# Sums of weight blocks moved to the second pass, and attention loads issued apart, in a fused attention and mixture-of-experts kernel

## The chip, the cores and the metric

One Trainium2 chip, of which the kernel uses one core. The time is that of one execution of the whole program on the device, in microseconds (us), the median of the runs shown. Engines: TensorE (PE in the profile), VectorE (DVE), ScalarE (ACT), GpSimd (POOL) and SyncE (SP), which here issues DMAs only. GpSimd issues DMAs too, from a queue of its own.

## What is computed

Attention within chunks of 64 tokens (batch 4, 8 heads, 576 tokens, head size 64), whose output is 2304 rows of 512 numbers; then two mixture-of-experts layers over these rows. The first sends every row through all four experts, weighted by given probabilities; the second sends each row through the one of eight experts that its logits choose.

```python
attn = softmax(scale * q_c @ k_c.T) ; x = attn @ v_c            # 64-token chunks, 8 heads
p = domain_probs / domain_probs.sum(-1)                          # first layer, E = 4
x = sum(p[:, e:e+1] * (relu(x @ w1[e]) @ w2[e]) for e in range(4))
e = argmax(x @ w_gate) ; g = softmax(x @ w_gate)[e]              # second layer, E = 8
out = g * (relu(x @ w1[e]) @ w2[e])                              # F = 1024, D = 512
```

## The kernel before

**Numbers as pairs.** Every operand of the large products is split into a high part (`wh`, `xh`, `hh`, cast by ScalarE to fp32r) and a low part (`wl`, `xl`, `hl`, the remainder, by VectorE); a product is three matmuls. A weight chunk is 128 x 1024: 512 columns of w1 and 512 of w2. It is loaded by SyncE into one of four raw buffers (`load_next`, L339), copied by ScalarE (L388) and subtracted by VectorE (L389) into one of eight pairs (`split_next`, L382). `feed` (L409) is called once per chunk or third of a unit: it issues the loads that have a free buffer and one or two splits. All orders are those of the program: each engine and each DMA queue works its list in order, and an instruction that waits holds up all behind it.

**Passes.** The 18 tiles of 128 rows go in five groups of 2, 4, 4, 4 and 4. The first pass (32 chunks, group 0) works the first layer plainly: per chunk a first product of 12 matmuls of 256 columns (L442 to L444) and a second one of 6 of 512 columns (L502), one chunk or two later. The four later passes use a scheme with seven products instead of eight (`unit`, L1011): 16 units per pass, each with three chunks, called kinds: kind 0 holds blocks of the weights themselves, kind 1 four sums and differences of them, kind 2 two chunks of w2. A unit has 42 matmuls of 256 columns (L1006) and 24 of 512 (L1094); the latter are woven into the next unit. GpSimd adds one pair of partial results in each (L1057).

**The sums.** `w_sums` (L371) is called in the first pass after every second split. GpSimd makes four sums of 128 x 256 from two raw chunks (L376 to L379) into `scr` or `xsum` and stores them to the DRAM tensor `wsum` (L380, 512 KB, GpSimd's queue). In all four later passes kind 1 is loaded from `wsum`. Since the sums read two raw chunks, loads in the first pass go in pairs: `done -= done % 2` (L418). At the pass's end GpSimd also makes the sums of the activations (`x_sums`, L284, L291), which ScalarE and VectorE split (`x_split`, L293).

**Attention** is done a group ahead, in pieces spread over the pass (`plan`, L948). `att_load` (L159) loads queries and keys of a tile (`atkq`, 512 KB, two buffers) and values (`atv`, 256 KB, four buffers). At the start tiles 0 to 3 are loaded; later, when the values of tile t are done, `attq` (L279) takes tile t + 4, due two calls of `feed` later, or at once in the first pieces, and both its loads are issued together (L923, L1032). A load whose buffer is not yet free waits on SyncE's queue.

**Routing.** Work beside the products stands in generators (`sides`), of which `side` (L909) takes a step at each call: `logits` (L523), then `route` (L559) with the exponential on ScalarE (L583), the ranks by a small matmul (L594), slot numbers on VectorE (L605) and an indirect store of each row's number and weight to `slots` by GpSimd (L608). In the last stage (the second layer, blocks of 256 rows, `step`, L1192, eight chunks each) the last group's routing and the tables (`tables`, `rest`: small matmuls L787 and L801, short VectorE instructions) take two steps per chunk in the first two blocks (L1216). In the second block, at its third chunk, SyncE fetches the slots of the next block (L845), two chunks later GpSimd gathers its rows (L850), and after the first product of the last chunk TensorE transposes them (`prep`, L861).

Of the kernel before, what the change touches and what calls it, by code (L numbers as in the profile page):

```python
# [9 lines left out]
F32 = mybir.dt.float32  # L10
# [4 lines left out]
ALU = mybir.AluOpType  # L15
# [3 lines left out]
P = 128  # L19
NT = 2304  # L20
NTILE = NT // P
# [35 lines left out]
LOWS = (9, 13)  # L57


@with_exitstack  # L60
def attn_moe_moe2(ctx, tc, att, probs, wg, wgt, w12, m2w, out):
# [94 lines left out]
    atin = {}  # L156
    attq = []

    def att_load(t, parts=((0, 1024), (1024, 1536))):  # L159
        if t not in atin:  # L160
            atin[t] = (
                apool.tile([P, 1024], F32, tag="atkq", name=f"atkq{t}", bufs=NKQ),
                apool.tile([P, 512], F32, tag="atv", name=f"atv{t}", bufs=NATT),
            )
        for c in parts:
            to = atin[t][0][:, c[0]:c[1]] if c[1] <= 1024 else atin[t][1]
            nc.sync.dma_start(out=to, in_=att[t, :, c[0]:c[1]])
# [29 lines left out]
    def att_scores(t, half):  # L197

        a = atin[t][0]
        if half == 0:  # L200
            live[t] = [
                sds[t % 2],
                apool.tile([P, 2, H], F32, tag="mx", name=f"mx{t}"),
                None,
            ]
        if half == 0 or t < GROUPS[0]:
            live[t][2] = ps("m").rearrange("p (h x) -> p h x", x=CH)
        sd, mx, sc = live[t]
        for g in range(4 * half, 4 * half + 4):
            for c in (slice(0, CH), slice(CH, P)):  # L210


                nc.tensor.matmul(
                    sc[other(c), g, :], lhsT=a[c, 512 + g * CH:512 + (g + 1) * CH], rhs=a[c, g * CH:(g + 1) * CH],
                    start=True, stop=True,
                )
            yield
        if heads(t, half):
            hs, n = heads(t, half)
            nc.vector.tensor_reduce(out=mx[:, 0, hs].unsqueeze(2), in_=sc[:, hs, :], axis=AX.X, op=ALU.max)  # L220
            nc.vector.tensor_tensor(
                out=sd[:, hs, 0:CH], in0=sc[:, hs, :], in1=mx[:, 0, hs].unsqueeze(2).to_broadcast([P, n, CH]),
                op=ALU.subtract,
            )
            nc.scalar.activation(sd[:, hs, 0:CH], sd[:, hs, 0:CH], AF.Exp, scale=0.125)

# [20 lines left out]
    def att_values(t, half, g):  # L247
        a = atin[t][1]
# [26 lines left out]
        if half == 1:  # L275
            live.pop(t)
            atin.pop(t)
            if t + NATT < NTILE:
                attq.append((t + NATT, stream["call"] + 2 if stream["call"] else 0))  # L279
# [4 lines left out]
    def x_sums(g):  # L284

        summed.append(g)
# [52 lines left out]
    def load_next():  # L339
# [28 lines left out]
    kept = []  # L368
    summed = []

    def w_sums(i, one, two):  # L371

        a11, a12, a21, a22 = one[:, 0:HN], one[:, HN:2 * HN], two[:, 0:HN], two[:, HN:2 * HN]
        to = (scr[:, 0:4, :], xsum.rearrange("p a k n -> p (a k) n")[:, 0:4, :])[0 if 1 in summed else i % 2]
        s1, s2, s3, s4 = [to[:, k, :] for k in range(4)]
# [4 lines left out]
        nc.gpsimd.dma_start(out=wsum[i * P:(i + 1) * P, :], in_=to.rearrange("p k n -> p (k n)"))  # L380

    def split_next():  # L382
# [4 lines left out]
        n = 768 if NPLAIN <= j < NM1 and (j - NPLAIN) % 3 == 0 else 1024  # L387
        nc.scalar.copy(wh[:, :n], raw[:, :n])  # L388
        lows.append(lambda: nc.vector.tensor_tensor(  # L389
            out=wl[:, :n], in0=raw[:, :n], in1=wh[:, :n].bitcast(F32), op=ALU.subtract  # L390
        ))
# [17 lines left out]
    def feed():  # L409
# [149 lines left out]
    def route(g, lg, wait):  # L559
# [359 lines left out]
    def chunk(j, x, sizes, fc, banks, frees, done, extra=()):  # L919
# [3 lines left out]
        while attq and attq[0][1] <= stream["call"]:  # L923
            att_load(attq.pop(0)[0])
# [24 lines left out]
    for g in range(1, len(GROUPS)):  # L949
        pcs = att_pieces(g)  # L950
        then = [lambda g=g: x_sums(g)] + [lambda g=g: x_split(g)] * (7 if g == 1 else 2)
# [59 lines left out]
    def unit(g, e, q, before, banks):  # L1011
# [19 lines left out]
        def extra(i):  # L1031
            while attq and attq[0][1] <= stream["call"]:  # L1032
                att_load(attq.pop(0)[0])
            feed()
            for p in plan.get(at + i, []):
                p()
            side()

        product(a, wa, 0, x["b11"], True, False)
# [20 lines left out]
        product(b, wa, HN, x["b21"], True, True)  # L1060
# [4 lines left out]
        product(a, wa, 2 * HN, x["t4"], False, True)  # L1065
# [40 lines left out]
    att_load(1, ((0, 1024),))  # L1106
    for t in range(2):
        att_load(t, ((1024, 1536),))
# [11 lines left out]
    for t in range(3, NATT):  # L1120
        att_load(t)
# [10 lines left out]
    for i, p in enumerate(pieces):  # L1132
# [5 lines left out]
        p()  # L1138
        keep_warm(WARM[1 + i])
# [52 lines left out]
    def step(s, c, sizes):  # L1192
# [11 lines left out]
        for fc in range(KF):  # L1204
# [6 lines left out]
            if s <= NFIRST:  # L1211
# [3 lines left out]
                else:  # L1215
                    side(2 if s < 2 else 1)  # L1216
# [84 lines left out]
```

## Time and profile before

| | |
|---|---|
| runs | 1181.06, 1181.13, 1183.89 us; median 1181.13 |
| profiled execution, its own time | 1183.33 us |
| its span, first to last instruction | 1181.3 us |
| TensorE busy | 1118.8 us, 95% of the span |
| VectorE, ScalarE, GpSimd busy | 761.4, 635.5, 255.3 us |
| mean granted TensorE clock | 0.98 of full speed |
| moved by DMA | 206.27 MB, 175 GB/s |

A busy TensorE is one that has matmuls in work; how fast they go depends on the clock granted, so a stretch is read with both. Idle time of an engine that is not the bottleneck costs nothing. The time behind an arrow in brackets is how long the engine stood idle before an instruction, and which instruction released it.

### The profile page before, as it was taken

The numbers are of one execution on the slowest core, as the hardware profiler recorded it, in microseconds if no ns is written. First come the engines' busy times: TensorE is split into PE (matmuls) and PEld (weight loads), VectorE is DVE, ScalarE is ACT, GpSimd is POOL, SyncE is SP. The second block draws the span as 40 slices with busy tenths as digits, with TensorE's granted clock in tenths as the row PEclk, the third lists the DMA queues.
The fourth block names the chain that finished last, engine by engine and source line by source line (L and its number), as shares of the span: only waits on it lengthen the run. The fifth ranks groups of instructions, "written<-read, shape, count | busy, mean of one in ns | idle before, by whom it ended". The sixth has DMA issues, their size and how long they took to land. (4 is left out here: it accounts for less than half of the span.)

```text
span 1181.3 us, 21164 instructions
## 1 busy us (share of the span) xinstructions
PE 1118.8 (95%) x7957; PEld 992.9 (84%) x7957; DVE 761.4 (64%) x1360; ACT 635.5 (54%) x1165; POOL 255.3 (22%) x291
## 2 busy tenths in 40 slices
PE   6699699999999999999999999999998999999996
PEld 4599589888888889898898898899986899788885
DVE  6577666576764666775665774675657566788871
ACT  3355356554655445555554565645444355677771
POOL 4476501000211200210210210120013111222220
PEclk9699999999999999999999999999999999999998
DMA  6688554534544464453344354354642486586850
GB/s 243 209 316 307 188 169 139 174 126 156 167 165 139 116 163 145 155 183 111 105 130 147 114 173 142 117 150 144 226 162 89 159 324 211 201 278 240 290 194 19
DMA packets 83905, 206.27 MB, mean 175 GB/s; under 512 B 13262, under 2 KB 22606, under 8 KB 83792
## 3 DMA queue, kind: packets, MB, share of 16 engines
q1 hardware_dynamic: 75536, 180.14, 46.3%
q0 software_dynamic: 8256, 24.67, 6.0%
q8 instruction: 65, 1.06, 0.4%
q14 instruction: 48, 0.39, 0.1%
HBM read 185.68 MB, written 20.27 MB: 174 GB/s over the span
## 5 line engine op out<-in xcount | busy, mean ns | idle before, releaser
L389 DVE TENSOR_TENSOR wl<-raw,wh 128x1024 fp32r<-128x1024 f32 (+1 forms) x276 | 332.5, 1206 | 120.8 <-ACT wh L388 120.7
L388 ACT CAST wh<-raw 128x1024 fp32r<-128x1024 f32 (+1 forms) x276 | 275.0, 997 | 28.5 <-DMA raw<-in_w 28.4
L1006 PE MATMUL ps_h<-xh,wh 128*128 128x256 f32 x896 | 258.7, 289 | 9.9 <-DVE hl L448 4.7
L1006 PE MATMUL ps_h<-xl,wh 128*128 128x256 f32 x896 | 253.3, 283 | 0.0
L1006 PE MATMUL ps_h<-xh,wl 128*128 128x256 f32 x896 | 252.6, 282 | 0.0
L1094 PE MATMUL ps_o<-wh,hh 128*128 128x512 f32 x512 | 201.5, 394 | 0.0
L1094 PE MATMUL ps_o<-wh,hl 128*128 128x512 f32 x512 | 201.5, 394 | 0.0
L1094 PE MATMUL ps_o<-wl,hh 128*128 128x512 f32 x512 | 201.0, 393 | 0.0
L1006 PEld LDWEIGHTS ps_h<-xh,wh 128*128 128x128 f32 x896 | 169.8, 189 | 24.6 <-ACT scr L1048 5.4
L1057 POOL TENSOR_TENSOR scr<-scr 128x256 f32<-128x256 f32 x64 | 58.1, 907 | 569.5 <-ACT scr L1056 569.3
L1006 PEld LDWEIGHTS ps_h<-xl,wh 128*128 128x128 f32 x896 | 169.5, 189 | 8.2
L1006 PEld LDWEIGHTS ps_h<-xh,wl 128*128 128x128 f32 x896 | 170.8, 191 | 0.0
L1068 ACT ACTIVATE hh<-scr 128x512 fp32r<-128x512 f32 (+1 forms) x128 | 66.7, 521 | 128.3 <-DVE scr L1061 126.1
L502 PE MATMUL ps_o<-wh,hh 128*128 128x512 f32 x328 | 124.6, 407 | 0.0
L1094 PEld LDWEIGHTS ps_o<-wh,hl 128*128 128x128 f32 x512 | 96.5, 188 | 21.6
L502 PE MATMUL ps_o<-wl,hh 128*128 128x512 f32 (+1 forms) x272 | 106.9, 397 | 0.0
L1094 PEld LDWEIGHTS ps_o<-wh,hh 128*128 128x128 f32 x512 | 97.1, 190 | 11.4
L1094 PEld LDWEIGHTS ps_o<-wl,hh 128*128 128x128 f32 x512 | 96.9, 189 | 11.2
L1069 DVE SCALAR_TENSOR_TENSOR hl<-scr,hh 128x512 fp32r<-128x512 f32 (+1 forms) x128 | 74.7, 584 | 44.8 <-ACT hh L1068 44.8
L1061 DVE TENSOR_TENSOR scr<-ps_h,scr 128x256 f32<-128x256 f32 x64 | 27.2, 424 | 93.9 <-PE ps_h L1006 93.8
L447 ACT ACTIVATE hh<-ps_h 128x256 fp32r<-128x256 f32 x80 | 30.7, 383 | 89.0 <-PE ps_h L444 83.0
L448 DVE SCALAR_TENSOR_TENSOR hl<-ps_h,hh 128x256 fp32r<-128x256 f32 x80 | 33.7, 421 | 66.0 <-ACT hh L447 64.3
(230 smaller groups left out, 1932.9 us busy)
## 6 DMA issues: line engine op xcount, KB each, us to landing
raw<-in_w SPq DMA_DIRECT2D x96, 512.0 KB
raw<-wsum SPq DMA_DIRECT2D x64, 512.0 KB
raw<-in_m2w SPq DMA_DIRECT2D x52, 512.0 KB
raw<-in_w SPq DMA_DIRECT2D x64, 256.0 KB
xraw<-in_m2w SPq DMA_DIRECT2D x28, 512.0 KB
atkq<-in_att SPq DMA_DIRECT2D x17, 512.0 KB
raw<-in_w SPq DMA_DIRECT2D x64, 128.0 KB
xsum<-in_m2w SPq DMA_DIRECT2D x13, 512.0 KB
```

Source lines behind the costliest of these rows:

```text
L388: nc.scalar.copy(wh[:, :n], raw[:, :n])
L389: lows.append(lambda: nc.vector.tensor_tensor(out=wl[:, :n], in0=raw[:, :n], in1=wh[:, :n].bitcast(F32), op=ALU.subtract))
L447: nc.scalar.activation(hh, hp[:, :n], AF.Relu)
L448: nc.vector.scalar_tensor_tensor(out=hl, in0=hp[:, :n], scalar=0.0, in1=hh.bitcast(F32), op0=ALU.max, op1=ALU.subtract)
L502: nc.tensor.matmul(y, lhsT=l, rhs=r, start=(fc == 0 and q == 0), stop=(fc == KF - 1 and q == len(parts) - 1))
L1006: nc.tensor.matmul(out, lhsT=l[:, c], rhs=r[:, k, :], start=first and k + q == 0, stop=last and k == 1 and q == 2, skip_group_check=True,)
L1057: nc.gpsimd.tensor_tensor(out=s3, in0=s3, in1=s5, op=ALU.add)
L1061: nc.vector.tensor_tensor(out=both[:, 0, :], in0=b, in1=s1, op=ALU.add)
L1068: nc.scalar.activation(h[0][:, c], src, AF.Relu)
L1069: nc.vector.scalar_tensor_tensor(out=h[1][:, c], in0=src, scalar=0.0, in1=h[0][:, c].bitcast(F32), op0=ALU.max, op1=ALU.subtract)
L1094: nc.tensor.matmul(banks[i], lhsT=l[:, c], rhs=r[:, d], start=q + f + k == 0, stop=q == NPAIRS - 1 and f == 1 and k == 2,)
```

## The change

1. `w_sums` is called in the second pass (group 1) instead of the first, when kind 0 of a unit is split; it takes all four blocks from one raw chunk (which is loaded in full there, 2 x 256 KB, with its halves in another order) and writes the sums straight into the raw buffer of kind 1, which is not loaded in that pass. The store to `wsum` goes from that buffer. Later passes load kind 1 as before. The pairing of the loads is gone.
2. Queries and keys are queued on their own, one call after the scores that free the buffer; values two calls after the values that free theirs. At the start the values of tiles 2 and 3 come before, their queries and keys after pieces 1 and 5 of the first group.
3. `route` yields before and after its exponential; the last stage takes two steps per chunk only in the first six chunks of its first block, then one.

```diff
+KEYS = {1: 2, 5: 3}
...
+    def att_load(t, parts=((0, 1024),)):
+        if t not in atkq:
+            atkq[t] = apool.tile([P, 1024], F32, tag="atkq", name=f"atkq{t}", bufs=NKQ)
         for c in parts:
+            nc.sync.dma_start(out=atkq[t][:, c[0]:c[1]], in_=att[t, :, c[0]:c[1]])
+    def att_load_v(t):
+        atv[t] = apool.tile([P, 512], F32, tag="atv", name=f"atv{t}", bufs=NATT)
+        nc.sync.dma_start(out=atv[t], in_=att[t, :, 1024:1536])
+    def att_loads():
+        for q in [q for q in attq if q[2] <= stream["call"]]:
+            attq.remove(q)
+            q[0](q[1])
...
+        if half == 1:
+            atkq.pop(t)
+            if NKQ <= t + NKQ < NTILE and t >= GROUPS[0]:
+                attq.append((att_load, t + NKQ, stream["call"] + 1))
...
             if t + NATT < NTILE:
-                attq.append((t + NATT, stream["call"] + 2 if stream["call"] else 0))
+                attq.append((att_load_v, t + NATT, stream["call"] + 2))
...
             if kind == 0:
-                parts = [(raw[:, 0:512], w12[e, 2 * q, :, 0:512]), (raw[:, 512:768], w12[e, 2 * q + 1, :, 256:512])]
+                c = 0 if u < E1 * NPAIRS else HN
+                parts = [(raw[:, 512:1024], w12[e, 2 * q, :, 0:512]), (raw[:, c:512], w12[e, 2 * q + 1, :, c:512])]
+            elif kind == 1 and u < E1 * NPAIRS:
+                parts = []
...
+    def w_sums(i, raw, to):
+        a21, a22, a11, a12 = [raw[:, k * HN:(k + 1) * HN] for k in range(4)]
+        s1, s2, s3, s4 = [to[:, k * HN:(k + 1) * HN] for k in range(4)]
         nc.gpsimd.tensor_tensor(out=s1, in0=a21, in1=a22, op=ALU.add)
         nc.gpsimd.tensor_tensor(out=s3, in0=a11, in1=a21, op=ALU.subtract)
         nc.gpsimd.tensor_tensor(out=s2, in0=s1, in1=a11, op=ALU.subtract)
         nc.gpsimd.tensor_tensor(out=s4, in0=a12, in1=s2, op=ALU.subtract)
+        nc.gpsimd.dma_start(out=wsum[i * P:(i + 1) * P, :], in_=to)
...
-        n = 768 if NPLAIN <= j < NM1 and (j - NPLAIN) % 3 == 0 else 1024
+        c = slice(HN if NPLAIN <= j < NM1 and (j - NPLAIN) % 3 == 0 else 0, 1024)
...
-        if j < NPLAIN:
-            if j % 2:
-                w_sums(j // 2, kept.pop(), raw)
-            else:
-                kept.append(raw)
+        if NPLAIN <= j < NPLAIN + 3 * E1 * NPAIRS and (j - NPLAIN) % 3 == 0:
+            while stream["load"] <= j + 1:
+                load_next()
+            w_sums((j - NPLAIN) // 3, raw, raws[j + 1][0])
+            raws[j + 1] = (raws[j + 1][0], stream["call"])
...
-                if stream["load"] < NPLAIN + NRAW:
-                    done -= done % 2
...
         nc.vector.tensor_tensor(out=sh, in0=lg, in1=mx.to_broadcast([P, n, E2]), op=ALU.subtract)
+        yield
         nc.scalar.activation(sh, sh, AF.Exp)
+        yield
...
-    att_load(2)
     nc.sync.dma_start(out=pr_raw, in_=probs)
     nc.sync.dma_start(out=wg_raw, in_=wg)
+    att_load_v(2)
+    att_load_v(3)
...
-    for t in range(3, NATT):
-        att_load(t)
...
         p()
+        if i in KEYS:
+            att_load(KEYS[i])
...
-                    side(2 if s < 2 else 1)
+                    side(2 if s == 0 and fc < 6 else 1)
```

## Rows read from the trace of the kernel before

**Rows 1.** Busy time by stretch: span, then busy us (instructions) by engine, clock, DMA.

```profile
core 0: us, PE busy (x) PEld busy (x) DVE busy (x) ACT busy (x) POOL busy (x), PEclk, DMA share, GB/s
25.40:52.40 27.00, 12.99 (x73) 11.27 (x73) 13.02 (x15) 5.52 (x8) 10.41 (x12) 0.62 0.58 196
52.40:132.30 79.90, 79.84 (x737) 71.67 (x735) 61.81 (x81) 41.40 (x67) 57.54 (x59) 1.00 0.76 262
132.30:152.00 19.70, 9.69 (x44) 8.62 (x44) 10.21 (x12) 8.29 (x15) 5.43 (x5) 0.83 0.83 286
...
147.50:332.00 184.50, 183.75 (x1383) 163.93 (x1384) 119.67 (x189) 103.03 (x195) 22.49 (x24) 0.99 0.48 154
```

**Rows 2.** TensorE's timeline: start, duration, instruction, idle before and releaser.

```profile
28.73 0.58 PE L442 MATMUL ps_h<-xh,wh 128*128 128x256 f32 x1 [3.17 <-DVE hl L448]
...
46.65 0.58 PE L442 MATMUL ps_h<-xh,wh 128*128 128x256 f32 x1 [10.84 <-DVE hl L448]
...
137.66 0.58 PE L442 MATMUL ps_h<-xh,wh 128*128 128x256 f32 x1 [5.32 <-DVE hl L448]
...
147.51 0.57 PE L1006 MATMUL ps_h<-xh,wh 128*128 128x256 f32 x1 [4.69 <-DVE hl L448]
```

**Rows 3.** SyncE's DMA queue, 33 to 60 us.

```profile
33.61 0.33 SPq L167 DMA_DIRECT2D atkq<-in_att  x1
33.98 0.43 SPq L167 DMA_DIRECT2D atv<-in_att  x1
34.58 24.56 SPq L364 DMA_DIRECT2D raw<-in_w  x10
```

**Rows 4.** Splits in the first pass on VectorE and ScalarE.

```profile
21.27 4.63 DVE L389 TENSOR_TENSOR wl<-raw,wh 128x1024 fp32r<-128x1024 f32 x2 [0.51 <-ACT wh L388]
...
113.12 1.23 DVE L389 TENSOR_TENSOR wl<-raw,wh 128x1024 fp32r<-128x1024 f32 x1 [0.52 <-ACT wh L388]
...
39.67 1.04 ACT L388 CAST wh<-raw 128x1024 fp32r<-128x1024 f32 x1 [11.45 <-DMA raw<-in_w]
```

**Rows 5.** End of the first pass, GpSimd and ScalarE.

```profile
128.42 1.06 POOL L379 TENSOR_TENSOR scr<-raw,scr 128x256 f32<-128x256 f32 x1
...
134.23 0.83 ACT L388 CAST wh<-raw 128x768 fp32r<-128x768 f32 x1 [8.78 <-DMA raw<-in_w]
```

**Rows 6.** TensorE: what follows twelve slow matmuls, and one chunk at full clock.

```profile
31.59 1.97 PE L213 MATMUL ps_m<-atkq 64*64 64x64 f32 x32
...
112.24 0.28 PE L442 MATMUL ps_h<-xh,wh 128*128 128x256 f32 x1
...
113.66 0.39 PE L502 MATMUL ps_o<-wh,hh 128*128 128x512 f32 x1
...
115.04 0.28 PE L442 MATMUL ps_h<-xh,wh 128*128 128x256 f32 x1
```

**Rows 7.** A routing step in the third pass, TensorE and ScalarE.

```profile
391.85 0.39 PE L1006 MATMUL ps_h<-xh,wh 128*128 128x256 f32 x1 [1.89 <-ACT scr L1048]
...
391.30 0.23 ACT L583 ACTIVATE sh<-sh 128x32 f32<-128x32 f32 x1 [4.00 <-DVE sh L582]
```

**Rows 8.** Routing in the last stage, by engine; last the page's gather, us to landing.

```profile
910.16 0.20 PE L787 MATMUL ps_m<-ident,tab 128*25 128x8 f32 x2 [3.27 <-DVE base L724]
...
918.05 0.81 PE L801 MATMUL ps_m<-lt,runs 25*128 25x18 f32 x6 [2.42 <-DVE lt L795]
...
898.79 0.17 DVE L605 CAST sloti<-slot 128x4 int32<-128x4 f32 x1
...
910.04 0.39 SPq L845 DMA_DIRECT2D slot_next<-slots  x1
...
914.74 1.02 POOL L850 DMA_INDIRECT yb<-ytok,src  x1 [0.30 <-DVE wl L389]
...
yb<-ytok,src POOLq DMA_INDIRECT x26, 6.6
```

**Rows 9.** One unit of the second pass; last the page's store of sums, us to landing.

```profile
269.52 0.69 DVE L1069 SCALAR_TENSOR_TENSOR hl<-scr,hh 128x512 fp32r<-128x512 f32 x1 [0.70 <-ACT hh L1068]
...
271.71 0.39 PE L1094 MATMUL ps_o<-wh,hh 128*128 128x512 f32 x1
...
wsum<-scr POOLq DMA_DIRECT2D x9, 512.0 KB, 6.4
```

More of the change, by code (lines that the diff above doesn't have):

```diff
@@ L154, in attn_moe_moe2 @@
     apool = attpool.enter_context(tc.tile_pool(name="att", bufs=2))
-    atin = {}
+    atkq, atv = {}, {}
     attq = []
[L159 to L164, printed above, removed]
-        for c in parts:
-            to = atin[t][0][:, c[0]:c[1]] if c[1] <= 1024 else atin[t][1]
-            nc.sync.dma_start(out=to, in_=att[t, :, c[0]:c[1]])
+    def att_load(t, parts=((0, 1024),)):
+        if t not in atkq:
+            atkq[t] = apool.tile([P, 1024], F32, tag="atkq", name=f"atkq{t}", bufs=NKQ)
+        for c in parts:
+            nc.sync.dma_start(out=atkq[t][:, c[0]:c[1]], in_=att[t, :, c[0]:c[1]])
[6 more added lines that the diff above has]
+            q[0](q[1])
     starts = [sum(GROUPS[:i]) for i in range(len(GROUPS))]
@@ L197, in att_scores @@
     def att_scores(t, half):
-        a = atin[t][0]
+        a = atkq[t]
         if half == 0:
@@ L247, in att_values @@
     def att_values(t, half, g):
-        a = atin[t][1]
+        a = atv[t]
         if g not in xs:
@@ L366, in load_next @@
         stream["load"] += 1
[L368 to L375, printed above, removed]
+    def w_sums(i, raw, to):
+        a21, a22, a11, a12 = [raw[:, k * HN:(k + 1) * HN] for k in range(4)]
+        s1, s2, s3, s4 = [to[:, k * HN:(k + 1) * HN] for k in range(4)]
         nc.gpsimd.tensor_tensor(out=s1, in0=a21, in1=a22, op=ALU.add)
@@ L379, in w_sums @@
         nc.gpsimd.tensor_tensor(out=s4, in0=a12, in1=s2, op=ALU.subtract)
-        nc.gpsimd.dma_start(out=wsum[i * P:(i + 1) * P, :], in_=to.rearrange("p k n -> p (k n)"))
+        nc.gpsimd.dma_start(out=wsum[i * P:(i + 1) * P, :], in_=to)
     def split_next():
@@ L386, in split_next @@
         wl = ring(wpool, "wl", NW, [P, 1024], F32R)
-        n = 768 if NPLAIN <= j < NM1 and (j - NPLAIN) % 3 == 0 else 1024
-        nc.scalar.copy(wh[:, :n], raw[:, :n])
+        c = slice(HN if NPLAIN <= j < NM1 and (j - NPLAIN) % 3 == 0 else 0, 1024)
+        nc.scalar.copy(wh[:, c], raw[:, c])
         lows.append(lambda: nc.vector.tensor_tensor(
-            out=wl[:, :n], in0=raw[:, :n], in1=wh[:, :n].bitcast(F32), op=ALU.subtract
+            out=wl[:, c], in0=raw[:, c], in1=wh[:, c].bitcast(F32), op=ALU.subtract
         ))
         wts[j] = (wh, wl)
-        if j < NPLAIN:
-            if j % 2:
-                w_sums(j // 2, kept.pop(), raw)
-            else:
-                kept.append(raw)
+        if NPLAIN <= j < NPLAIN + 3 * E1 * NPAIRS and (j - NPLAIN) % 3 == 0:
[3 more added lines that the diff above has]
+            raws[j + 1] = (raws[j + 1][0], stream["call"])
         stream["split"] += 1
@@ L922, in chunk @@
             split_lows()
-        while attq and attq[0][1] <= stream["call"]:
-            att_load(attq.pop(0)[0])
+        att_loads()
         h = ffn1(j, x, sum(sizes))
@@ L950, in attn_moe_moe2 @@
         pcs = att_pieces(g)
-        then = [lambda g=g: x_sums(g)] + [lambda g=g: x_split(g)] * (7 if g == 1 else 2)
+        then = [x_sums] + [lambda g=g: x_split(g)] * (7 if g == 1 else 2)
         begin, end = begins[g - 1], begins[g] - (0 if g == 1 else NSUB)
@@ L1031, in extra @@
         def extra(i):
-            while attq and attq[0][1] <= stream["call"]:
-                att_load(attq.pop(0)[0])
+            att_loads()
             feed()
@@ L1037, in extra @@
             side()
-        product(a, wa, 0, x["b11"], True, False)
+        product(a, wa, 512, x["b11"], True, False)
         nc.scalar.copy(s1, a)
@@ L1059, in unit @@
         before[2]()
-        product(b, wa, HN, x["b21"], True, True)
+        product(b, wa, 768, x["b21"], True, True)
         nc.vector.tensor_tensor(out=both[:, 0, :], in0=b, in1=s1, op=ALU.add)
@@ L1064, in unit @@
             hs.append((ring(hpool, "hh", LAG + 2, [P, 512], F32R), ring(hpool, "hl", LAG + 2, [P, 512], F32R)))
-        product(a, wa, 2 * HN, x["t4"], False, True)
+        product(a, wa, HN, x["t4"], False, True)
         def activate(h, c, src):
@@ L1105, in attn_moe_moe2 @@
     att_load(0, ((0, 512), (512, 1024)))
-    att_load(1, ((0, 1024),))
+    att_load(1)
     for t in range(2):
-        att_load(t, ((1024, 1536),))
+        att_load_v(t)
     for _ in range(NRAW):
         load_next()
-    att_load(2)
     nc.sync.dma_start(out=pr_raw, in_=probs)
     nc.sync.dma_start(out=wg_raw, in_=wg)
+    att_load_v(2)
+    att_load_v(3)
     nc.gpsimd.memset(wg_sb, 0.0)
```

5 lines of the change are left out of this document (2 added, 3 removed).

## The prediction

> **What bounds the kernel now.** I read the stretches first. In the first pass, once it runs, TensorE is busy all the time at full clock, 79.84 of 79.90 us [rows 1]: there only fewer columns could help. The stretches on either side are another matter: 12.99 busy of 27.00 us at a mean granted clock of 0.62 before it, 9.69 of 19.70 at 0.83 behind it [rows 1]. TensorE's own idle times say where: 3.17 and 10.84 us early in the pass, 5.32 and 4.69 us at its end [rows 2], 24.0 us in all, and after each wait the matmuls run at the lower of the clock's two levels, 1.2 instead of 2.4 GHz. The releaser named is VectorE's low half of an activation, but what that stood behind is seen one view further on. The reader should follow two chains.
>
> At the start it is SyncE's queue. The queries and keys of the sixth tile, L167, are issued only at 33.61, when the scores that free their buffer have run; ten weight loads stand behind them and begin at 34.58 [rows 3]. ScalarE waits 11.45 us for the first of them and starts its copy at 39.67 [rows 4]. The smaller gap before it is VectorE's: two low halves took 4.63 us beside GpSimd's sums, 1.23 us each alone [rows 4].
>
> At the end of the pass it is GpSimd. Its fourth weight sum, L379, ends at 129.48; it was the last reader of a raw buffer, so the next load goes out then, and ScalarE, idle for 8.78 us, copies at 134.23 [rows 5]. The gap of 4.69 us is the same chain one pair later.
>
> **First pass, start.** The change issues later keys and values one or two calls after the scores or values that free their buffer, so no weight load stands behind a wait. Removed: 3.17 + 10.84 = 14.0 us idle. The lower clock also goes: twelve matmuls take 2.86 us there (28.73 to 31.59) and 1.42 at full clock (112.24 to 113.66) [rows 2, 6]; two such groups and as much again of second products and scores give about 4.8 us. What is late next is VectorE: with 1.23 us for each low half its queue ends 2.2 us earlier, so of 3.17 about 1 us stays, and a like wait follows a chunk later while the splits catch up: I leave 2.3 us. Gain 16.5; ends 12 (lower clock stays) and 18.8 (no wait left).
>
> Loads by pair become loads one by one; a raw buffer is then free at VectorE's low half. A chunk takes 2.80 us (112.24 to 115.04) [rows 6], four buffers give 11.2 us for load (4.75 us, from 129.48 to 134.23 [rows 5]), low half (1.23) and copy (taken as long): 7.2. Covered. The values of the third and fourth tile, the probabilities and the gate weights, go ahead of the keys now; none waits for a buffer, cost nothing.
>
> **First pass, end.** The 64 sums and 16 stores leave this pass; GpSimd has only the four x sums left. Removed: 5.32 + 4.69 = 10.0 us, and some 3.0 us of lower clock (1.44 us for the first twelve matmuls behind each gap). ScalarE's copies now wait for the first sums of the second pass; I keep 1 us for that. Gain 12; ends 8 and 13.
>
> **Second pass.** Each of 16 units loses one 512 KB load and gains 128 KB; four sums and the 512 KB store stand on GpSimd behind L1057. A unit takes 184.5 / 16 = 11.5 us [rows 1]. The sums take 4 x 1.06 = 4.2 us at the shared price of L379 [rows 5]; ScalarE's copy of their result comes a third of a unit, 3.8 us, after the split that orders them, so at most 0.4 us a unit shows, and GpSimd can start before ScalarE does, since it need only see the load. Without that cover 16 x 0.4 = 6 us. Behind it, SyncE's load into the stored buffer now waits for the store, 6.4 us [rows 9], and all loads stand behind that. The loop sums 4.2, store 6.4, load 4.75, and 3 us for copy, low half and issues is 18.4 us, and has two units, 23.1 us. Loss 0 to 8, taken as 1, nearest to the covered end.
>
> A second price is VectorE's. What a row shows: low halves nearly double beside GpSimd's sums [rows 4]. The first low half of a unit ends at 270.21 and is read by the third matmul of the group that begins at 271.71 [rows 9], two steps of 1.38 / 6 us later [rows 6], at 272.17: slack 1.96 us. I take no stall. The Trainium skill, page "SBUF — State Buffer", section "Who interferes with whom", says that a VectorE instruction with two SBUF inputs and a GpSimd instruction reading SBUF exclude each other for a whole instruction. The trace's 4.63 us agrees. By it the two low halves of a unit that read SBUF twice could each wait a whole sum, which is the third rival below.
>
> **Routing.** The yields put the exponential a call behind its input. ScalarE stood 4.00 us for that input, and TensorE 1.89 us behind ScalarE's copy [rows 7]; a second wait of the same size stands one pass later. Gain 3.8; ends 2 and 4.5. In the last stage one routing step per chunk replaces two. The waits of 3.27 and 2.42 us [rows 8] go, 5.7 us. But the slot numbers come later: the step that makes them moves from the seventh chunk of the first block to the first chunk of the second. From slot numbers (L605, 898.79) to the slot fetch on SyncE (910.04), second gather (914.74) and its landing (6.6 us) takes 22.5 us [rows 8]. TensorE transposes the gathered rows after eight first and five second products of the block, 8 x 1.42 + 5 x 1.38 = 18.3 us [rows 6], while slot numbers are there at best 1.42 + 2 us in (the 2 us chosen for one activation and its short steps): 25.9 us. A new wait of some 7 us. The lower clock behind it I price like that behind the old ones. Net -1; ends -6 and +7.
>
> **Sum.** 16.5 + 12 - 1 + 3.8 - 1 = 30.3 us. Against the profiled execution: 1183.33 - 30.3 = 1153.0, its span 1181.3 - 30.3 = 1151.0. Its own time lies 2.2 us above the median 1181.13, so for the median 1150.8, say **1151**.
>
> **Rivals.** (1) *Slower: the second pass starves on its store.* Place: the load behind the store. It costs from a loop above 23.1 us and turns the sign above 23.1 + 2 x 30.3 / 16 = 26.9. If store and load took twice their rows, the loop is 29.6, each unit 3.3 us longer, 16 x 3.3 = 52 us: 1203. Against: both were measured in a fuller DMA stretch (0.76 and 0.83 busy) than the second pass has (0.48) [rows 1]. 4%. (2) *The start is not the queue's.* If the early loads land no sooner, because the DMA engines are filled by the first five tiles, or VectorE keeps the pace, only some 3 us of the 16.5 come: 1164. Against: the DMA share is 0.58 there [rows 1]. 8%. (3) *VectorE's low halves in the second pass.* Two waits of one sum (1.06) make 2.1 us against 1.96, 2 us in all; of one and a half sums each 3.2, 1.2 a unit, 20 us. The middle, 11 us, gives 1162. 10%. (4) *The routing wait is dearer or the load behind the fetch is late:* 1157 to 1161. 13%. (5) *No gather wait and nothing lost at the end of the pass:* 1141 to 1144. 13%. (6) *The change does not do what it says:* other waits take the place of those removed at both ends, 1178 to 1184. 2%.
>
> **How the numbers follow.** The forecast's own case, 1145 to 1156, has 50%. The range 1141 to 1162 takes in cases 3 to 5, together 86%, of which I count some 6 as tails beyond its ends; it leaves out cases 1, 2 and 6. A difference of 0.3%, 3.5 us, is about what a measurement can tell from no change. Faster 0.95, same 0.02, slower 0.03 follow from cases 1 and 6.
>
> **What would show it.** Right: weight loads on SyncE from about 15 us on without a gap of 10 us; TensorE with no idle time over 2 us between 20 and 130 us and a clock near 1.00; second pass begun some 28 us earlier and lasting 184 to 186 us; no 1.89 us waits; a wait at L861 of 4 to 8 us in the second block of the last stage in place of those at L787 and L801. Wrong: a SyncE queue waiting for the store with ScalarE waiting for raw in the second pass, its length above 190 us, or a gap of more than 5 us left before 50 us.

## The result, and the profile after

| | before | after |
|---|---|---|
| runs taken together on one chip, median | 1182.51 us (4 runs, 1181.06 to 1184.77) | 1147.07 us (4 runs, 1145.65 to 1150.37) |
| ratio | | 0.9703, 95% interval 0.9674 to 0.9731 |
| profiled execution, own time; span | 1183.33; 1181.3 | 1145.65; 1143.9 |
| TensorE busy | 1118.8, 95% | 1103.9, 96% |
| VectorE, ScalarE, GpSimd busy | 761.4, 635.5, 255.3 | 757.8, 634.5, 248.0 |
| mean granted clock | 0.980 | 0.996 |
| moved by DMA | 206.27 MB | 199.97 MB |

The changed kernel is 35.4 us faster by the medians, 37.7 by the two profiled executions. The lines of the code have moved by 4 to 8; the correspondences are given as they come up.

**The start.** TensorE's timeline after the change, two rows of the first pass (start, duration, instruction, idle before and releaser), which answer to [rows 2]:

```profile
26.51 0.39 PE L448 MATMUL ps_h<-xh,wh 128*128 128x256 f32 x1 [1.09 <-DVE hl L454]
31.28 0.38 PE L448 MATMUL ps_h<-xh,wh 128*128 128x256 f32 x1 [0.40 <-DVE hl L454]
```

Of the 3.17 and 10.84 us before, 1.09 and 0.40 are left. SyncE's queue after the change, against [rows 3]:

```profile
10.33 1.60 SPq L164 DMA_DIRECT2D atkq<-in_att  x2
14.86 14.82 SPq L376 DMA_DIRECT2D raw<-in_w  x6
29.77 0.86 SPq L168 DMA_DIRECT2D atv<-in_att  x2
30.68 0.42 SPq L164 DMA_DIRECT2D atkq<-in_att  x1
32.38 6.32 SPq L376 DMA_DIRECT2D raw<-in_w  x3
```

Six weight loads go out from 14.86 us on, where ten stood behind keys until 34.58; the later keys, one issue at a time, hold nobody. Busy time by stretch (span, then busy us and instructions of PE, PEld, DVE, ACT, POOL; granted clock; DMA share; GB/s), after the change:

```profile
0.00:34.00 34.00, 24.07 (x285) 19.95 (x287) 22.55 (x43) 14.85 (x24) 3.68 (x28) 1.00 0.74 259
0.00:35.00 35.00, 25.07 (x291) 20.83 (x293) 23.51 (x44) 14.85 (x24) 3.68 (x28) 1.00 0.75 262
32.00:110.00 78.00, 78.00 (x732) 70.85 (x731) 60.43 (x87) 42.51 (x69) 11.57 (x9) 1.00 0.69 236
864.40:894.40 30.00, 24.95 (x167) 21.68 (x165) 23.73 (x90) 13.89 (x22) 9.89 (x9) 1.00 0.41 142
```

and before, with the block of the last stage that answers to the last row above:

```profile
0.00:52.40 52.40, 30.14 (x288) 25.13 (x289) 28.69 (x44) 15.18 (x24) 21.16 (x48) 0.80 0.64 223
898.40:933.10 34.70, 28.72 (x166) 24.92 (x167) 23.69 (x98) 11.99 (x19) 9.44 (x9) 0.90 0.43 152
```

The count of matmuls places the same work in both traces, to within a few records: the 288 that were done at 52.4 us are now done between 34 and 35, about 34.5. That is 17.9 us. From 32 to 110 us TensorE has no idle time at all, at full clock.

**Where the rest went.** The start of GpSimd's add of partial results (L1057 before, L1063 after) marks each unit; the first one of each pass, the last one, and the transposes of the last stage (L861, L869) cut the profiled executions into stretches (us):

| kernel | to second pass | 2nd | 3rd | 4th | 5th | to first transposes | first to third transposes | rest |
|---|---|---|---|---|---|---|---|---|
| before | 156.38 | 175.76 | 185.40 | 183.60 | 163.54 | 33.68 | 58.00 | 224.94 |
| after | 125.00 | 177.82 | 182.21 | 181.93 | 164.75 | 32.66 | 54.97 | 224.56 |
| loads together | 136.64 | 177.89 | 182.16 | 181.89 | 164.78 | 32.66 | 56.15 | 224.53 |
| sums in first pass | 147.65 | 175.80 | 182.27 | 181.94 | 164.78 | 32.66 | 56.56 | 224.54 |
| routing undone | 126.19 | 178.13 | 183.76 | 183.61 | 163.54 | 33.68 | 57.97 | 224.22 |
| no store | 127.46 | 177.69 | 182.20 | 181.93 | 164.78 | 32.66 | 54.97 | other data |
| no sums | 124.62 | 175.83 | 182.19 | 181.94 | 164.76 | 32.66 | 56.34 | other data |
| two steps in first block | 126.03 | 177.90 | 182.17 | 181.91 | 164.74 | 32.66 | 51.57 | 228.42 |
| yields undone | 124.38 | 178.11 | 185.36 | 181.80 | 163.58 | 32.95 | 51.53 | 224.29 |
| scatter later | 125.30 | 177.88 | 181.00 | 180.30 | 163.45 | 32.66 | 51.58 | 224.23 |
| sums earlier | 129.13 | 175.32 | 181.08 | 180.33 | 163.45 | 32.54 | 51.59 | 224.66 |

The three kernels without the yields differ by 1.6 to 1.8 us in their third pass (185.40 and 185.36 against 183.76) and in their fourth (183.60 and 183.61 against 181.80); the run with the yields undone shows below that this is the granted clock. Up to the second pass 31.4 us are gained, in the second 2.1 lost, in the third to fifth 3.7 gained, in the last stage 4.4 (1.0 + 3.0 + 0.4).

TensorE's idle times over 0.7 us between the end of the first pass and the third block of the last stage, after the change:

```profile
128.06 0.39 PE L1013 MATMUL ps_h<-xh,wh 128*128 128x256 f32 x1 [0.97 <-DVE hl L1075]
266.44 0.39 PE L1013 MATMUL ps_h<-xh,wh 128*128 128x256 f32 x1 [0.86 <-ACT scr L1046]
381.77 0.39 PE L1013 MATMUL ps_h<-xh,wh 128*128 128x256 f32 x1 [0.92 <-ACT scr L1046]
564.61 0.39 PE L1013 MATMUL ps_h<-xh,wh 128*128 128x256 f32 x1 [1.35 <-ACT scr L1046]
741.69 0.38 PE L1013 MATMUL ps_h<-xh,wh 128*128 128x256 f32 x1 [0.74 <-ACT scr L1046]
879.19 0.39 PE L448 MATMUL ps_h<-x,wh 128*128 128x256 f32 x1 [0.85 <-DVE hl L454]
883.63 0.39 PE L448 MATMUL ps_h<-x,wh 128*128 128x256 f32 x1 [1.37 <-DVE hl L454]
893.11 0.66 PE L869 MATMUL ps_m<-ident,yb 128*128 128x128 f32 x4 [2.19 <-DMA yb<-ytok,src]
```

The 5.32 and 4.69 us at the end of the first pass [rows 2] are down to one of 0.97. The two of 1.89 us [rows 7] are gone, but three smaller ones stand behind another ScalarE copy (L1046, L1040 before). In the last stage the 3.27 and 2.42 us [rows 8] are gone, and the wait for the gathered rows stands in their place, 2.19 us and 0.64 for the second half.

### The profile page after: what moved, and what is told of

Its sections match the earlier page's. It is cut to its first block, busy times and chain, and to the rows that moved or that the text cites. A ratio compares the mean times of both kernels' runs of the same rounds, so it can differ in the third digit from the quotient of the medians.

```text
span 1143.9 us, 21116 instructions
## 1 busy us (share of the span) xinstructions
PE 1103.9 (96%) x7956; PEld 980.5 (86%) x7957; DVE 757.8 (66%) x1360; ACT 634.5 (55%) x1165; POOL 248.0 (22%) x291
## 2 busy tenths in 40 slices
DMA packets 81600, 199.97 MB, mean 175 GB/s; under 512 B 13006, under 2 KB 20302, under 8 KB 81488
## 5 line engine op out<-in xcount | busy, mean ns | idle before, releaser
L397 DVE TENSOR_TENSOR wl<-raw,wh 128x1024 fp32r<-128x1024 f32 (+1 forms) x276 | 326.9, 1186 | 92.9 <-ACT wh L396 92.7
L1013 PE MATMUL ps_h<-xh,wh 128*128 128x256 f32 x896 | 258.0, 288 | 6.4 <-ACT scr L1046 4.3
L1013 PE MATMUL ps_h<-xl,wh 128*128 128x256 f32 x896 | 252.4, 282 | 0.0
L1013 PE MATMUL ps_h<-xh,wl 128*128 128x256 f32 x896 | 251.6, 281 | 0.0
L1100 PE MATMUL ps_o<-wh,hh 128*128 128x512 f32 x512 | 200.8, 392 | 0.0
L1100 PE MATMUL ps_o<-wh,hl 128*128 128x512 f32 x512 | 200.7, 392 | 0.0
L1100 PE MATMUL ps_o<-wl,hh 128*128 128x512 f32 x512 | 200.2, 391 | 0.0
L1013 PEld LDWEIGHTS ps_h<-xh,wh 128*128 128x128 f32 x896 | 168.7, 188 | 21.2 <-ACT scr L1046 6.7
L1013 PEld LDWEIGHTS ps_h<-xl,wh 128*128 128x128 f32 x896 | 168.5, 188 | 8.0
L1013 PEld LDWEIGHTS ps_h<-xh,wl 128*128 128x128 f32 x896 | 169.9, 190 | 0.0
L1063 POOL TENSOR_TENSOR scr<-scr 128x256 f32<-128x256 f32 x64 | 59.1, 924 | 498.9 <-ACT scr L1062 485.0
L1074 ACT ACTIVATE hh<-scr 128x512 fp32r<-128x512 f32 (+1 forms) x128 | 66.7, 521 | 137.7 <-DVE scr L1067 127.7
L1075 DVE SCALAR_TENSOR_TENSOR hl<-scr,hh 128x512 fp32r<-128x512 f32 (+1 forms) x128 | 79.3, 620 | 53.3 <-ACT hh L1074 53.3
L1100 PEld LDWEIGHTS ps_o<-wh,hl 128*128 128x128 f32 x512 | 96.1, 188 | 21.3
L1100 PEld LDWEIGHTS ps_o<-wh,hh 128*128 128x128 f32 x512 | 96.8, 189 | 11.3
L1100 PEld LDWEIGHTS ps_o<-wl,hh 128*128 128x128 f32 x512 | 96.4, 188 | 11.1
```

The source lines that it names most:

```text
L397: lows.append(lambda: nc.vector.tensor_tensor(out=wl[:, c], in0=raw[:, c], in1=wh[:, c].bitcast(F32), op=ALU.subtract))
L1013: nc.tensor.matmul(out, lhsT=l[:, c], rhs=r[:, k, :], start=first and k + q == 0, stop=last and k == 1 and q == 2, skip_group_check=True,)
L1063: nc.gpsimd.tensor_tensor(out=s3, in0=s3, in1=s5, op=ALU.add)
L1074: nc.scalar.activation(h[0][:, c], src, AF.Relu)
L1075: nc.vector.scalar_tensor_tensor(out=h[1][:, c], in0=src, scalar=0.0, in1=h[0][:, c].bitcast(F32), op0=ALU.max, op1=ALU.subtract)
L1100: nc.tensor.matmul(banks[i], lhsT=l[:, c], rhs=r[:, d], start=q + f + k == 0, stop=q == NPAIRS - 1 and f == 1 and k == 2,)
```

## The experiments

All are changes of the changed kernel. The ratios are to the kernel before, run beside them on the same chip: 1183.25 us for the first four, 1180.89 for the next four, 1181.60 for the last three. The changed kernel was run beside the first and the last group, not beside the middle one. The stretches and waits of a run are those of one profiled execution.

**The changed kernel again.** No edit.

> The changed kernel once more, beside the next three on the same chip. Every theory: 1145 to 1150 us, ratio to the kernel before 0.967 to 0.973. It is the line from which the three undone parts are counted.

1147.54 us, ratio 0.9709 (0.9688 to 0.9730). The gain repeats.

**Loads together** undoes part 2 alone.

```diff
-                attq.append((att_load_v, t + NATT, stream["call"] + 2))
+                attq.append((att_both, t + NATT, stream["call"] + 2 if stream["call"] else 0))
...
-        if i in KEYS:
-            att_load(KEYS[i])
```

> Only the attention loads undone: queries, keys and values of a tile issued together again, due as before. Theory: weight loads stand behind a load that waits for its buffer, so a gap of about 10 us and the low clock behind it come back between 30 and 50 us: 1160 to 1166 us. Rival: the gap was made by GpSimd's sums in the first pass (they hold the raw buffers and slow VectorE's low halves), which stay out here: at most 1151 us.

1160.18 us, ratio 0.9823 (0.9796 to 0.9849): 12.6 us worse. The long gap is back; two rows, TensorE's and ScalarE's timelines of this run:

```profile
41.15 0.58 PE L450 MATMUL ps_h<-xh,wh 128*128 128x256 f32 x1 [11.10 <-DVE hl L456]
...
35.64 1.04 ACT L398 CAST wh<-raw 128x1024 fp32r<-128x1024 f32 x1 [10.45 <-DMA raw<-in_w]
```

and its SyncE queue:

```profile
28.51 0.33 SPq L164 DMA_DIRECT2D atkq<-in_att  x1
28.88 0.43 SPq L168 DMA_DIRECT2D atv<-in_att  x1
29.42 29.65 SPq L378 DMA_DIRECT2D raw<-in_w  x13
```

With no sums in the first pass, a queue that waits for one tile's keys still gives the whole gap (10.84 before, 11.10 here). The rival that has the DMA engines too full for earlier loads is out.

**Sums in the first pass** undoes part 1 alone.

```diff
+        if j < NPLAIN:
+            if j % 2:
+                w_sums(j // 2, kept.pop(), raw)
+            else:
+                kept.append(raw)
```

> Only the place of the sums undone: GpSimd makes them in the first pass again, and kind 1 is loaded in all four later passes. Theory: the two gaps at the end of the first pass come back with their low clock (10 + 3 us), some 2 us more early in the pass from slower low halves, and the second pass gets 2 us shorter: 1158 to 1163 us. Rival: the sums also made the long gap at the start: 1172 us or more.

1167.02 us, ratio 0.9872 (0.9843 to 0.9901): 19.5 us worse, more than expected. The gaps at the pass's end are back, and none over 1.62 us at the start:

```profile
124.00 0.58 PE L452 MATMUL ps_h<-xh,wh 128*128 128x256 f32 x1 [4.46 <-DVE hl L458]
...
137.48 0.58 PE L1017 MATMUL ps_h<-xh,wh 128*128 128x256 f32 x1 [6.97 <-DVE hl L458]
```

```profile
36.90:110.00 73.10, 72.12 (x690) 64.98 (x689) 58.76 (x77) 39.28 (x64) 50.79 (x55) 1.00 0.87 305
110.00:148.00 38.00, 25.29 (x126) 21.59 (x126) 19.07 (x23) 13.29 (x24) 15.66 (x16) 0.78 0.53 176
```

By stretches (the same columns as above): 1 us idle between 37 and 110, a DMA share of 0.87 instead of 0.69, and 12.7 us idle behind 110 at a granted clock of 0.78. By the count of first products the sixth chunk starts at 36.91 us (34.63 after the change) and the twenty-sixth at 100.81 (97.23): 2.3 us are lost at the start, 1.3 in the middle and some 19 at the end. So the queue makes the long gap, the sums those at the end. The second pass is 2.0 us shorter without them (175.80).

**Routing undone** undoes part 3 alone, yields and steps.

```diff
-        yield
         nc.scalar.activation(sh, sh, AF.Exp)
-        yield
...
-                    side(2 if s == 0 and fc < 6 else 1)
+                    side(2 if s < 2 else 1)
```

> Only the routing undone: no yields beside the exponential, two steps per chunk in both first blocks of the last stage. Theory: two waits of 1.9 us in the later passes and the waits of 3.3 and 2.4 us with low clock behind them come back: 7 to 9 us, 1154 to 1156 us. Rival (the forecast's own sum): the last stage's steps are worth nothing, only the yields' 3 to 4 us: 1150 to 1151 us.

1152.76 us, ratio 0.9757 (0.9733 to 0.9781): 5.2 us worse, between the two. The waits of 1.89 us are back, and in the last stage

```profile
880.70 0.54 PE L793 MATMUL ps_m<-ident,tab 128*25 128x8 f32 x4 [3.36 <-DVE base L730]
888.59 0.81 PE L807 MATMUL ps_m<-lt,runs 25*128 25x18 f32 x6 [2.49 <-DVE lt L801]
```

The three undone parts add up to 12.6 + 19.5 + 5.2 = 37.3 us, against 35.7 for all at once (1183.25 - 1147.54).

**No store.**

```diff
-        nc.gpsimd.dma_start(out=wsum[i * P:(i + 1) * P, :], in_=to)
...
-                parts = [(raw, wsum[at:at + P, :])]
+                parts = [(raw, w12[e, 2 * q])]
```

> Leaves out the store of the sums in the second pass; the three later passes read kind 1 from the weights themselves (512 KB each, as many bytes as before), so their kind 1 holds other numbers. Theory (the store holds a raw buffer of the queue, but nothing waits for it, since the loads of the second pass are a buffer ahead): second pass 177.8 us as before, its idle times of 0.97, 0.34 and 0.86 us stay, total 1146 to 1148. Rival (the store's hold on its buffer, 2.9 us to landing, is what makes the second pass 2 us longer): second pass about 175.8, total about 1145.

1162.41 us, ratio 0.9846 (0.9829 to 0.9862), but that total says nothing: other numbers route the rows otherwise, and the last stage has one more block of 19.3 us (13 sets of transposes instead of 12), which the expectation overlooked. The passes take no branch on the data: the second takes 177.69 us, against 177.82 with the store. The hold on the buffer is covered.

**No sums.** As above, and `w_sums` gone with the full load of kind 0.

> Leaves out sums and store altogether; kind 1 is read from the weights in all four later passes, and kind 0 with 768 columns in the second too. Theory (GpSimd's sums beside VectorE's low halves are the whole cost of the second pass): second pass back to about 175.8 us as in the kernel before, no idle time of over 0.3 us in it, the low half of 128x512 at about 0.69 us in place of up to 1.23; total about 1145. Rival (the longer second pass comes from the later phase of attention's pieces and loads, not from the sums): second pass stays at 177 to 178, total 1147.

1162.37 us, ratio 0.9849 (0.9832 to 0.9866), with the same extra block. The second pass is back at 175.83. One wait of 0.43 is left of its three. VectorE's low halves of the activations, grouped by shape from 128 to 303 us after the change (busy, mean ns):

```profile
L1075 DVE SCALAR_TENSOR_TENSOR hl<-scr,hh 128x512 fp32r<-128x512 f32 x15 | 12.8, 852 | 10.5 <-ACT hh L1074 10.5
L1075 DVE SCALAR_TENSOR_TENSOR hl<-scr,hh 128x256 fp32r<-128x256 f32 x16 | 9.6, 599 | 0.0
L1075 DVE SCALAR_TENSOR_TENSOR hl<-ps_h,hh 128x256 fp32r<-128x256 f32 x16 | 6.6, 414 | 0.0
```

and in the run without sums, 127 to 302 us:

```profile
L1067 DVE SCALAR_TENSOR_TENSOR hl<-scr,hh 128x512 fp32r<-128x512 f32 x15 | 11.3, 756 | 10.5 <-ACT hh L1066 10.5
L1067 DVE SCALAR_TENSOR_TENSOR hl<-scr,hh 128x256 fp32r<-128x256 f32 x16 | 7.4, 460 | 0.0
L1067 DVE SCALAR_TENSOR_TENSOR hl<-ps_h,hh 128x256 fp32r<-128x256 f32 x16 | 6.7, 416 | 0.0
```

So the 2.0 us of the second pass go with the sums, and the two forms that read SBUF twice are slower beside them (852 against 756 ns, 599 against 460), the one that reads PSUM is not. The edit brings the loads of kind 1 back as well; that the sums are the cause is seen where single low halves meet them. GpSimd's and VectorE's timelines after the change:

```profile
260.45 0.74 POOL L386 TENSOR_TENSOR raw<-raw,raw 128x256 f32<-128x256 f32 x1
...
260.55 1.18 DVE L1075 SCALAR_TENSOR_TENSOR hl<-scr,hh 128x512 fp32r<-128x512 f32 x1 [0.70 <-ACT hh L1074]
...
239.54 0.69 DVE L1075 SCALAR_TENSOR_TENSOR hl<-scr,hh 128x512 fp32r<-128x512 f32 x1 [0.70 <-ACT hh L1074]
```

The first low half begins 0.64 us before the end of the sum that is running and takes 0.49 us more than 0.69; the second begins 0.08 us before the end of one (L386, to 239.62) and takes 0.69. So it is in all 14 units of the changed kernel's second pass in which GpSimd is at work then: a low half that starts inside one of GpSimd's instructions is longer by what is left of that one, less some 0.14 us.

**Two steps in the first block.**

```diff
-                    side(2 if s == 0 and fc < 6 else 1)
+                    side(2 if s == 0 else 1)
```

> Two steps in all eight chunks of the last stage's first block, where the changed kernel takes two in the first six. Theory (the gather's wait of 2.2 and 0.6 us hangs on the scatter of the slots, which now comes a chunk or two earlier): the wait before the transposes is under 0.5 us, total 1144 to 1146. Rival (the two more steps put a wait of TensorE on a short VectorE instruction in the place of the gather's, as in the kernel before with its 3.3 and 2.4 us): waits of 2 us or more before small matmuls of the routing, total 1147 to 1149.

1144.38 us, ratio 0.9687 (0.9669 to 0.9704), as expected, though the interval still touches the change's. First to third transposes take 51.57 us, where the changed kernel took 54.4 to 56.9 in three profiles; the gather is awaited no longer, and no wait over 0.7 us comes in its place in these two blocks. The rest of this profiled execution, the slowest of the five, is 3.9 us longer than after the change: the rows of a later block are awaited for 1.99 and 1.58 us (986.59, 988.83), with the lower clock behind. The later run with the same steps does not have this (224.23).

**Yields undone**, the number of steps left as changed.

```diff
-        yield
         nc.scalar.activation(sh, sh, AF.Exp)
-        yield
```

> The two yields around the exponential taken out, the number of steps per chunk left as changed. Theory (the yields give 1.6 and 1.7 us in the third and fourth pass and take 1.2 in the fifth; the last stage's gain of some 3 us is that of the fewer steps): third and fourth pass 183.8 and 183.6 us, the waits of 1.9 us back in them, fifth 163.5; last stage within 2 us of the changed kernel's; total 1148 to 1151. Rival (the yields earn all of the third part of the change, in the last stage too): total about 1152, last stage 3 us longer.

1144.24 us, ratio 0.9697 (0.9681 to 0.9713), where 1148 to 1151 were expected: no worse than the change (0.9709), by the middle values 1.4 us better. In the table the third to fifth pass lose 1.9 us without the yields (530.74 against 528.89), and the two blocks gain 3.4 (51.53 against 54.97). The waits of 1.9 us are back, and what they cost differs. Seven microseconds from each of them, in the kernel before, with routing undone and with the yields undone (columns as above, the granted clock third from last):

```profile
391.90:398.90 7.00, 7.00 (x58) 6.05 (x62) 3.90 (x10) 3.20 (x6) 1.23 (x1) 0.76 0.39 128
577.30:584.30 7.00, 7.00 (x40) 5.98 (x41) 3.53 (x9) 3.15 (x6) 0.83 (x1) 0.76 0.17 57
...
364.00:371.00 7.00, 6.30 (x98) 5.50 (x99) 5.11 (x11) 3.81 (x7) 1.24 (x1) 1.00 0.35 127
547.80:554.80 7.00, 6.98 (x39) 5.96 (x40) 3.53 (x9) 3.14 (x6) 0.84 (x1) 0.76 0.17 61
...
362.20:369.20 7.00, 7.00 (x53) 5.91 (x56) 3.53 (x9) 3.14 (x6) 1.15 (x1) 0.76 0.35 123
547.60:554.60 7.00, 7.00 (x52) 6.29 (x53) 5.04 (x13) 3.62 (x8) 1.24 (x1) 1.00 0.17 60
```

The clock fell behind four of the six, and these are the four longer passes of the table. So the loss of 1.9 us holds one fall of 1.6 to 1.8 us. With a fall in neither pass the same sum would be 183.76 + 181.80 + 163.58 = 529.14, only 0.2 us above that with the yields; with both, as before, it is 532.54.

A yield is a step too: with two less, the scatter of the slots comes earlier, and the rows are there in time. So in these profiles the yields as placed give back in the last stage what they earn in the passes. What part 3 earns in the last stage comes from the step count: without the yields, the old count (routing undone) takes 57.97 us for the two blocks, the new one 51.53.

**Scatter later**: two steps in the first block, and

```diff
         nc.vector.tensor_copy(sloti, slot.rearrange("p n o -> p (n o)"))
+        if g < len(GROUPS) - 1:
+            yield
```

> Two steps in all eight chunks of the first block, and one step more between the slot numbers and the scatter of the groups before the last. Theory (with the two yields GpSimd's four scatter instructions stand just ahead of its add of two partial results, 379.5 in place of some 374 us, and that late add is what TensorE waits for, 0.92 us in the third pass, 1.35 in the fourth, 0.74 in the fifth): these three waits go, the passes take 181.2, 180.6 and 164.0 us, total about 1141 to 1142 (3 us below the kernel with only the two steps). Rival (the add is late but another wait ends with it): the waits move to another instruction and the passes stay at 182.2, 181.9 and 164.8, total 1144.

1138.37 us, ratio 0.9642 (0.9621 to 0.9662), the best of all. The mechanism is as expected, the gain larger: third to fifth pass 524.75 us against 528.89, 4.1 us; the two steps in the first block give 3.4 more in the two blocks (51.58 against 54.97). GpSimd's timeline after the change, in the unit ahead of the wait at 381.77:

```profile
374.11 1.04 POOL L616 DMA_INDIRECT slots<-gt,sloti  x1 [10.10 <-DVE sloti L613]
...
378.53 0.97 POOL L616 DMA_INDIRECT slots<-gt,sloti  x1 [0.30 <-issue]
379.53 0.74 POOL L1063 TENSOR_TENSOR scr<-scr 128x256 f32<-128x256 f32 x1
```

and in this run:

```profile
374.35 0.74 POOL L1065 TENSOR_TENSOR scr<-scr 128x256 f32<-128x256 f32 x1 [9.96 <-ACT scr L1064]
375.25 1.04 POOL L618 DMA_INDIRECT slots<-gt,sloti  x1 [0.16 <-issue]
```

Four scatters with their issue took 5.4 us of GpSimd's program, and the add behind them came that much later; ScalarE waited 3.38 us for it (L1074), and TensorE 0.92 for the copy behind. In the third pass of the kernel before, the scatters stand ahead of the add too, but they begin 5 us before the copy that it needs (402.18; the copy ends at 407.52, the add starts at 407.81), while after the change they begin as that copy ends (373.91). With the scatters behind the add no such wait is left in the three passes.

**Sums earlier**, on top of the last.

```diff
+            if i == 1:
+                presum(j + 6)
```

(`presum` makes the sums of a unit two units ahead, before the add instead of behind it.)

> As the run with the later scatter, and GpSimd's sums of the second pass stand ahead of its add in each unit instead of behind it, so that they do not fall together with VectorE's low halves of the activations. Theory (the second pass is 2 us longer because these low halves take up to 1.23 us beside the sums): second pass 176 us, the three waits gone, total 2 us below the run with the later scatter. Rival (the add, now some 4 us later in every unit because the sums wait for their load, makes TensorE wait as the scatter did): waits of 0.2 to 0.6 us in most of the 16 units, second pass 180 to 186, total 1144 to 1150.

1139.76 us, ratio 0.9647 (0.9626 to 0.9668): no gain, neither theory. The table's 175.32 is no gain of the pass either, since the first mark came late itself (129.13). New waits stand in two units:

```profile
131.86 0.39 PE L1022 MATMUL ps_h<-xh,wh 128*128 128x256 f32 x1 [1.47 <-ACT scr L1057]
189.96 0.39 PE L1022 MATMUL ps_h<-xh,wh 128*128 128x256 f32 x1 [0.89 <-ACT scr L1057]
```

At the first, ScalarE waited 2.99 us for the add, which now stands behind the sums (it starts at 129.13). At the second a low half takes 1.48 us beside GpSimd's store and add, and the copy comes late behind VectorE's work. In the whole pass the waits over 0.1 us at the first products come to 3.72 us, against 2.45 after the change: the sums ahead of the add have moved the cost, not removed it.

**The changed kernel beside the last two.**

> The changed kernel unaltered, on the same chip as the two above: 0.970 to 0.972 of the kernel before, some 1147 us where that takes 1182. It is there so that the others are compared on one chip.

1147.06 us, ratio 0.9717 (0.9696 to 0.9739). On this chip the run with the later scatter is 8.7 us faster than the change.

## Why the prediction was right, and which term was off

Forecast 1151 in 1141 to 1162, measured 1147.07. The terms against the stretches of the two profiled executions:

| term | forecast, us gained | ends | measured |
|---|---|---|---|
| start of the first pass | 16.5 | 12 to 18.8 | 17.9 |
| end of the first pass | 12 | 8 to 13 | 13.5 (31.4 - 17.9) |
| second pass | -1 | -8 to 0 | -2.1 |
| exponential | 3.8 | 2 to 4.5 | 3.7 |
| routing, last stage | -1 | -6 to +7 | +4.4 |
| sum | 30.3 | | 37.4 |

Of the 37.4 us the medians show 35.4, since the profiled run of the changed kernel lies 1.4 us under its median and that of the kernel before 0.8 over its own.

**The two ends of the first pass** went as worked out, the second 0.5 us beyond its end. Both wait chains were the right ones, which undoing one part at a time shows. At the start the forecast's two groups of 1.44 us "and as much again" make 5.8 us, not the 4.8 that it adds, and the term 17.5. Of the waits there "about 1 us stays, and a like wait follows": 1.09 and 0.40, so that 2.3 us left in was 0.8 too much. Split by parts instead of places, the gain up to the second pass is 11.6 us for the loads (136.64 - 125.00) and 22.7 for the sums (147.65 - 125.00); each alone against the kernel before would be 8.7 and 19.7. Some 3 us belong to both.

**Second pass.** Twice the loss taken, 2.1 for 1, and for the other reason. The term was argued from the store and from the copy that waits for the sums; the store costs nothing. What costs is the price for which the prediction took no stall: low halves beside the sums. The rule of the Trainium skill, page "SBUF — State Buffer", section "Who interferes with whom", is borne out: only the forms with two inputs in SBUF got slower, and each by about the rest of the sum that it started in. A whole sum was never lost: at most 0.68 us were left of one, and in the mean a unit's two such low halves lose 0.10 + 0.14 us. The slack of 1.96 us was worked out for the wrong reader. It is that of the second products (L1094, now L1100), which wait nowhere in the pass. All waits over 0.2 us stand at the first products of the next unit (L1013): at 128.06 and 218.18 for the low half that reads PSUM, which stands behind the slow one on VectorE (it ends at 128.00 and 218.13), at 266.44 for a ScalarE copy (L1046) that came late behind VectorE's work. The waits over 0.1 us there come to 2.45 us with the sums and 0.77 without. The third rival had the right place and 11 us for a cost of 2.

**Routing in the last stage: the mis-sized term.** The prediction's step was "a new wait of some 7 us". The wait came, at L869 as said, and measured 2.19 + 0.64 = 2.83. Its chain after the change, VectorE, SyncE and GpSimd by their timelines:

```profile
872.53 0.17 DVE L613 CAST sloti<-slot 128x4 int32<-128x4 f32 x1
...
881.56 0.39 SPq L853 DMA_DIRECT2D slot_next<-slots  x1
...
886.38 1.02 POOL L858 DMA_INDIRECT yb<-ytok,src  x1 [0.30 <-DVE hl L454]
```

The block starts at 869.36, so the slot numbers come 3.2 us in (forecast 3.4). From there to the fetch it is 9.0 us (11.25 in [rows 8]), and TensorE is at the transposes at 893.11, 20.6 us behind the slot numbers instead of 22.5. TensorE itself was ready after 890.92 - 869.36 = 21.6 us, not 18.3; 0.85 and 1.37 us of that are other waits in the block, which the prediction did not have. The two together are 1.9 + 3.3 us and the 0.2 of the start, 5.4 in all, which is 7.6 - 5.4 = 2.2. Against the forecast that is 4.2 us less wait (7 - 2.83); the other two waits take 2.2, and the lower clock behind the old waits, two falls or some 3.4 us, has no successor: 4.2 - 2.2 + 3.4 = 5.4, the difference between -1 and 4.4. In the clock the profiled execution was lucky. The granted clock of that block was 0.90 before, with idle times of 3.27 and 2.42 us in it, and 1.00 after. The step "the lower clock behind it I price like that behind the old ones" was wrong for this execution, but not for the kernel: in the profile of the changed kernel taken again, the same wait, 2.57 us there, has the lower clock behind it (that run first, then the change):

```profile
893.40:900.40 7.00, 6.33 (x29) 4.73 (x30) 2.71 (x5) 1.69 (x4) 0.00 (x0) 0.76 0.55 209
...
893.10:900.10 7.00, 6.35 (x37) 5.05 (x38) 2.71 (x5) 2.57 (x5) 0.62 (x1) 1.00 0.59 223
```

The two blocks take 56.9 us in that profile, 54.97 in this one. The run with routing undone has waits of 3.36 and 2.49 us again, and 57.97 us for them.

**Exponential: right by luck.** The forecast's 3.8 us are the two waits of 1.89 us alone. These went, but two terms that it did not have nearly cancel: the lower clock behind both waits in the kernel before, some 3.4 us gained, and the three new waits behind GpSimd's add, 0.92 + 1.35 + 0.74 = 3.0 us lost. That makes 4.2 for 3.7 measured; the remaining 0.5 was not separated. Undoing the yields alone shows 1.9 us and not 3.7 because the clock fell once in that profile, not twice. The prediction worked out what stands behind a moved step on SyncE's queue, not what stands behind it on GpSimd's.

**The rivals.** The start was the queue's; the store did not starve the second pass; the routing wait was smaller than taken, not dearer; no waits of that size came in the place of those removed at the two ends. The case "no gather wait, nothing lost" (1141 to 1144) is about what the run with two steps in the first block gives (1144.38). Of the signs named, one failed: the wait at the transposes was to be 4 to 8 us.

**Open.** The 2.0 us of the second pass: placing the sums ahead of the add moved them only. What some 19 us at the end of the first pass in the sums' run are made of, beyond the two gaps and the lower clock, was not separated further. No run shows why the clock falls behind one wait and not behind another of the same length.

## What to carry to other kernels

A load that waits for its buffer on an in-order queue costs what stands behind it: issue it when the buffer is free and leave the queue to loads that can go. Work on an idle engine is dear where it holds a buffer in the stretch that waits for buffers, and cheap in one that doesn't (here 64 sums and 16 stores: some 20 us against 2). When steps of a generator are moved by a yield, look at every engine's list for what they now stand ahead of, and at the last step of the chain for what is now late: here both cost about what the yields earned, and the places of two steps together (the later scatter, two steps in the first block) were worth 8.7 us. Price a wait of TensorE with the lower clock that may follow, as a chance: here a fall cost nearly as much again as a wait of 1.9 us, and one profile does not tell whether it comes.

## What the runs showed of the hardware that was not expected

The clock falls behind short waits, and not each time: behind TensorE's waits of 1.9 us in four of six cases; behind the first wait for gathered rows in four of seven profiles (it fell behind 2.57, 2.50, 2.31 and 1.92 us, not behind 2.20, 2.19 and 1.40). A fall cost 1.6 to 1.8 us. A low half with two inputs in SBUF that started while GpSimd added was held for about the rest of that addition, up to 0.54 us in the second pass.

Landing times are not a property of the transfer alone: the scatter of slots took 4.6 us in the median after the change and 7.9 before (of 18 each, the landings of 13 and 8 are known), the store of sums 2.9 us in the second pass and 6.4 in the first [rows 9], where the DMA share was 0.76 and more [rows 1]; that the load of the DMA engines is the reason is not shown. An add of GpSimd that came over 5 us late cost TensorE 0.7 to 1.4 us a time, no more.
